# A second, turned copy of w_out for the product with the experts' gate

## The chip, the core and the metric

The kernel runs on one core of a Trainium2 chip. That core has a matrix engine (TensorE: PE for its matmuls, PEld for its weight loads), a vector engine (DVE), a scalar engine (ACT), a general engine (POOL) and a queue engine that issues DMAs (SP). The metric is the device time of one execution in microseconds.

## The reference

Three stages run one after the other. Random-feature attention gives `x`; a gated feed-forward block turns `x` into `h @ w_out`; a router then gives each of 2304 tokens to one of 8 experts, in order of the logits, and each expert has two more matrices.

```
q_p, k_p = phi(q * s), phi(k * s)               # exp of projections, 128 features
num = q_p @ (k_p^T v);  x = num / (q_p . sum k_p)
xn  = x / rms(x) * rms_g
h   = silu(xn @ w_gate) * (xn @ w_val)          # 2304 x 1536
y   = h @ w_out                                 # w_out: 1536 x 512, float64
logits = y @ moe2_w_gate                        # 512 x 8
# tokens to experts by descending logit, at most 288 per expert
out[mask_e] = relu(y[mask_e] @ w1[e]) @ w2[e]
```

`w_out` and the two gate matrices come as float64. The kernel reads their 64-bit words and makes float32 values on the chip.

## The kernel before

**Logits ahead of y.** The router needs the logits exactly and early, and `y` only later. So the kernel computes `wog = w_out @ moe2_w_gate` (1536 x 8) once, and gets the logits as `h @ wog` straight from `h`, as soon as a chunk of `h` is there (`ffn_lg`, L652, L653). `y` itself (L900) is computed afterwards, under the routing.

**Ticks.** `run_tick` (L758) writes one tick of work for each of 88 items: four batches of attention, each 12 items for keys (`KItem`) and 10 for queries (`QItem`). An item is spread over lags 0 to 5 of later ticks. Its TensorE work is projections (L367 to L369; without the split in batch 0, L372), transposes of the features (L454), products with values or keys (L413, L458) and a transpose of the normalised rows (L463). 576 queries make four tiles of 128 rows and one of 64, so in each batch there are two query items (the two halves of the heads) with 64 rows instead of 128; below they are called **half tiles**, and their L454, L458 and L463 read `64*128` or `128*64` in the profile. To each tick belongs one step of the feed-forward (`ffn_step_pe`, 24 matmuls of 256 columns, L596 to L598, called **FFN matmuls** below; 108 such steps in all).

**Conversion.** `useq` (L703) is the list of conversions: 24 `WgvUnit` and then 12 `WoUnit`, one for each chunk of 128 rows of `w_out`. `conv_pe` and `conv_el` move units through lags 0 to 3, one lag per tick; while they convert w_out they start one unit every second tick. All units do `load` (L519, 512 KB into one of three `ws` buffers), at lag 0 `magnitude` (L523, ACT) and at lag 1 `word` (L527, L528, L529, DVE) into one of three `dw` buffers. A `WoUnit` then

- at lag 1 writes the chunk to `wo_dr` in DRAM (L579), from which the product for `y` takes it later (`wo_split`, L816);
- at lag 2 transposes the chunk in four pieces on TensorE (L567) into a PSUM buffer `gv`, from which ACT copies it back over the chunk (L581);
- at lag 3 multiplies the turned chunk with the gate (L571, four matmuls of 8 columns) and puts the two halves of the result into `wog` (L583, L584). `ffn_step_pe` does not go on to a logit product before its chunk is in `wogs`.

The buffers `dw` are shared with `late_load` (L626), which brings the `h` of the first two blocks back for their logits, and the two `gv` buffers with the feed-forward steps.

**Order.** TensorE's order is as written for the first 27 ticks. After that a scheduler in the framework orders all engines' instructions, by priorities (attention ahead of the rest) and by when it expects buffers and operands; each engine then runs its own list strictly in that order.

Of the kernel before, what the change touches and what calls it, by code (L numbers as in the profile page):

```python
# [9 lines left out]
F32 = mybir.dt.float32  # L10
# [10 lines left out]
NT, DM, FF, E, FE = B * S, 512, 1536, 8, 1024  # L21
# [7 lines left out]
KD = DM // 128  # L29
KF = FF // 128  # L30
# [9 lines left out]
DW = 3  # L40
# [14 lines left out]
def const_f32():  # L55
    c = np.zeros((128, C_N), np.float32)
    i = np.arange(128)
    c[:, C_ID:C_SL] = np.eye(128)
    c[:, C_SL:C_SA] = np.arange(SL)
    c[:, C_SA:C_C] = np.arange(NSL)  # L60
    c[:, C_C:C_P] = np.arange(NC)
    c[:, C_P] = i
    c[:, C_E:C_T] = np.arange(E)
    e = np.arange(E)
    c[:, C_T:C_N] = (e[None, :] < e[:, None]).reshape(-1)
    return c


def triangles():
    i = np.arange(128)  # L70
    j = np.tile(np.arange(CAP), (128, 1))
    return np.concatenate([i[:, None] < i[None, :], i[:, None] >= i[None, :], j], 1).astype(np.float32)


def const_i32():
    rows = []
    for n, (d, s) in enumerate(zip(DIGITS, SHIFTS)):
        j = np.arange(1 if n else 2, 1 << d, dtype=np.uint32) << np.uint32(s)
        if n == 0:
            j = np.where(j >= 0x80000000, j ^ np.uint32(0x80000000), ~j)  # L80
        rows.append(j.astype(np.uint32))
    return np.tile(np.concatenate(rows).view(np.int32), (128, 1))
# [195 lines left out]


@with_exitstack  # L280
def kernel(ctx, tc, qT, kT, v1, om, wgv, rms, wo, wg2, w1, w2, cfd, trd, cid, out, dbg=None):
    nc = tc.nc
    dbg = dbg or {}
    keep = ctx.enter_context(tc.tile_pool(name="keep", bufs=1))
# [6 lines left out]
    wo_dr = dram.tile([KF, 128, DM], F32, name="wo_dr")  # L291

    cf = keep.tile([128, C_N], F32, name="cf")
    ident = cf[:, C_ID:C_SL]
# [14 lines left out]
    psG = ctx.enter_context(tc.tile_pool(name="psG", bufs=2, space=PSUM))  # L309
    mid = ExitStack()  # L310
    fp = mid.enter_context(tc.tile_pool(name="fp", bufs=2))
# [54 lines left out]
    def proj(pp, xh, xl):  # L366
        nc.tensor.matmul(pp, xh, omh, start=True, stop=False)  # L367
        nc.tensor.matmul(pp, xh, oml, start=False, stop=False)
        nc.tensor.matmul(pp, xl, omh, start=False, stop=True)  # L369

    def proj_whole(pp, x):
        nc.tensor.matmul(pp, x, oms, start=True, stop=True)  # L372
# [9 lines left out]
    class KItem:  # L382
        def __init__(self, b, p, g):
            self.b, self.p, self.g = b, p, g
            self.ts = [t for t in (2 * g, 2 * g + 1) if t < 5]
# [9 lines left out]
        def pe(self, lag):  # L395
            b, p, g = self.b, self.p, self.g
            if lag == 0:
                self.pp = psA.tile([128, 4, M], F32, name="pp", bufs=2)
                if b == 0:
                    for i, t in enumerate(self.ts):  # L400
                        proj_whole(self.pp[:, 2 * i:2 * i + 2, :], kts[b, p][:, t * 128:t * 128 + 128])
                    return
                kh, kl = khs.pop((b, p, g))
                for i, t in enumerate(self.ts):
                    proj(self.pp[:, 2 * i:2 * i + 2, :], kh[:, i * 128:i * 128 + 128], kl[:, i * 128:i * 128 + 128])
            elif lag == 1:
                if g == 0:
                    st["pk", b, p] = psA.tile([128, 512], F32, name="pm", bufs=3)
                pk = st["pk", b, p]
                vt = vts[b, p]  # L410
                for i, t in enumerate(self.ts):
                    for h in range(2):
                        nc.tensor.matmul(pk[:, h * (D + 1):(h + 1) * (D + 1)], self.ft[:, 2 * i + h, :], vt[:, t, h, :],  # L413
                                         start=(t == 0 and h == 0), stop=(t == 4), skip_group_check=True)

        def el(self, lag):
            b, p, g = self.b, self.p, self.g
            if lag == 0:
                self.ft = feat(self.pp, 128, 2 * len(self.ts))
            elif lag == 1 and g == 2:  # L420
                if p == 0:
                    kvs[b] = at.tile([128, H, D + 1], F32, name="kvs")
                nc.scalar.copy(kvs[b][:, 2 * p:2 * p + 2, :].rearrange("p h d -> p (h d)"),
                               st.pop(("pk", b, p))[:, :2 * (D + 1)])
# [129 lines left out]
                    gvs.add(f)  # L554

    class WoUnit(Unit):
        def __init__(self, f):
            self.f = f

# [1 line left out]
            return wo[self.f]  # L561

        def pe(self, lag):
            if lag == 2:
                self.pt = psG.tile([128, KD, 128], F32, name="gv")
                for k in range(KD):
                    nc.tensor.transpose(self.pt[:, k, :], self.t[:, k * 128:(k + 1) * 128], ident)  # L567
            elif lag == 3:
                self.pw = self.pt[:, 0, :E]
                for k in range(KD):  # L570
                    nc.tensor.matmul(self.pw, self.t[:, k * 128:(k + 1) * 128], wg2s[:, k, :], start=(k == 0), stop=(k == KD - 1))  # L571

        def el(self, lag):
            f = self.f
            if lag == 0:
                self.magnitude(fp.tile([128, DM], F32, name="dw", bufs=DW))
            elif lag == 1:
                self.word()
                nc.sync.dma_start(wo_dr[f], self.t)  # L579
            elif lag == 2:  # L580
                nc.scalar.copy(self.t, self.pt.rearrange("p k m -> p (k m)"))  # L581
            elif lag == 3:
                nc.vector.tensor_copy(wog[:, f, 0, :], self.pw)  # L583
                nc.vector.tensor_sub(wog[:, f, 1, :], self.pw, wog[:, f, 0, :])  # L584
                wogs.add(f)
# [104 lines left out]
    def ffn_step_el():  # L690
        if "el" in fst:
            j, f, pg = fst.pop("el")
            ffn_el(j, f, pg)
            ffn_rank_el()
            return j, f
        return None
# [3 lines left out]
    for b in range(B):  # L700
        items += [KItem(b, p, g) for p in range(4) for g in range(3)]
        items += [QItem(b, t, hf) for t in range(5) for hf in range(2)]
    useq = [WgvUnit(f, g) for f in range(KF) for g in range(2)] + [WoUnit(f) for f in range(KF)]  # L703
    AHEAD = 3


# [126 lines left out]
    while True:  # L833
        if not ffn_step_pe():
            break
        j, f = ffn_step_el()
# [223 lines left out]
def layouts(q, k, v, omega, moe_w_gate, moe_w_val, moe_w_out, moe_rms_g, moe2_w_gate, moe2_w1, moe2_w2):  # L1060
    a = np.asarray
    hp = H // 2

    def bits(x):
        return np.ascontiguousarray(x).view(np.int64)

    qT = a(q).reshape(B, hp, 2, S, D).transpose(0, 2, 4, 1, 3).reshape(B, 128, hp, S)
    kT = np.zeros((B, hp, 128, 640), np.float32)
    kT[..., :S] = a(k).reshape(B, hp, 2, S, D).transpose(0, 1, 2, 4, 3).reshape(B, hp, 128, S)
    v1 = np.zeros((B, hp, 2, 640, D + 1), np.float32)  # L1070
    v1[:, :, :, :S, :D] = a(v).reshape(B, hp, 2, S, D)
    v1[:, :, :, :S, D] = 1.0
    v1 = v1.reshape(B, hp, 2, 5, 128, D + 1).transpose(0, 1, 4, 3, 2, 5)
    om = np.zeros((128, 2 * M), np.float32)
    om[:D, :M] = a(omega).T
    om[D:, M:] = a(omega).T
    wgv = np.stack([bits(moe_w_gate), bits(moe_w_val)], 0).reshape(2, KD, 128, KF, 128).transpose(3, 2, 1, 0, 4)
    wgv = wgv.reshape(KF, 128, 1024)
    rms = np.tile(a(moe_rms_g)[None], (128, 1))
    wo = bits(moe_w_out).reshape(KF, 128, DM)  # L1080
    wg2 = a(moe2_w_gate).reshape(KD, 128, E).transpose(1, 0, 2)
    w1 = a(moe2_w1).reshape(E, KD, 128, 4, 256).transpose(0, 3, 2, 1, 4).reshape(E, 4, 128, 1024)
    w2 = a(moe2_w2).reshape(E, KE, 128, KD, 128).transpose(0, 3, 2, 1, 4).reshape(E, 4, 128, 1024)
    d = dict(qT=qT, kT=kT, v1=v1, om=om, wgv=wgv, rms=rms, wo=wo, wg2=wg2, w1=w1, w2=w2,
             cf=const_f32(), tri=triangles(), ci=const_i32())
    return {n: np.ascontiguousarray(x) for n, x in d.items()}

# [16 lines left out]
```

## Time and profile before

| | |
|---|---|
| median of 3 runs | 1002.11 us (1001.75 to 1002.58) |
| the profiled execution | 998.29 us, of which the span in the profile is 996.5 us |
| PE, PEld busy | 969.5 us (97%), 884.8 us (89%) |
| DVE, ACT, POOL busy | 535.7 us (54%), 399.3 us (40%), 243.7 us (24%) |
| DMA moved | 153.32 MB, mean 154 GB/s |

The span holds three parts: attention with the feed-forward up to about 545 us, routing with the product for `y` under it up to about 750 us, and the experts to the end. A PE row's "busy" is modelled and overlaps with its neighbours, so what a matmul costs is read from one start to the next. PE's idle time is shown by the profile only where a row carries `[idle <-releaser]`.

### The profile page before, as it was taken

What the parts mean: (1) busy time and instruction counts of PE and PEld (TensorE: products, weight loads), DVE (VectorE), ACT (ScalarE), POOL (GpSimd) and SP (SyncE); (2) the same over time, 40 slices, a digit from 0 to 9 for tenths busy, and PEclk for the clock granted to TensorE, in tenths of its full rate; (3) what the DMA queues carried; (4) which work ended last, traced back from release to release, by engine and by line L of the source; (5) the groups of instructions that cost most, each with busy time, mean ns of one, the idle gap of its engine ahead of it and who ended that gap; (6) DMA issues with size and microseconds to landing.
All of it is one profiled execution on the core that took longest, in us unless ns stands there. A gap on an engine that the chain in (4) does not pass through costs nothing.

```text
span 996.5 us, 19333 instructions
## 1 busy us (share of the span) xinstructions
PE 969.5 (97%) x7667; PEld 884.8 (89%) x7667; DVE 535.7 (54%) x1239; ACT 399.3 (40%) x999; POOL 243.7 (24%) x326
## 2 busy tenths in 40 slices
PE   9989999999999999999999999999997999999996
PEld 7788899999999989999999777777776999999996
DVE  4889956454553344432243555655565655555531
ACT  6976545555645545332243011010004544444420
POOL 2456412243444322322232000000005112122111
PEclk9999999999999999999999999999999999999999
DMA  8547744375344111712132666655527855555400
GB/s 299 159 141 234 226 132 125 111 257 199 131 141 155 67 54 51 223 80 86 79 145 107 190 184 178 189 173 166 163 72 239 251 187 183 186 196 198 149 24 24
DMA packets 112074, 153.32 MB, mean 154 GB/s; under 512 B 8560, under 2 KB 78832, under 8 KB 111984
## 3 DMA queue, kind: packets, MB, share of 16 engines
q1 hardware_dynamic: 108768, 142.52, 44.3%
q0 software_dynamic: 3072, 9.44, 2.9%
q8 instruction: 60, 0.98, 0.4%
q14 instruction: 30, 0.25, 0.1%
q10 hardware_dynamic: 144, 0.13, 0.0%
HBM read 108.03 MB, written 44.04 MB: 153 GB/s over the span
## 4 chain that ended last, share of the span: by engine, by line
PE 79%; issue 9%; DVE 6%; DMA 2%; POOL 2%; ACT 2%; POOLq 0%; DVEq 0%; ACTq 0%
PE py L900 16%; PE gv L596 10%; PE gv L597 10%; PE gv L598 9%; PE pm L458 3%; PE cnt L164 2%; PE pm L413 2%; PE py L998 2%; PE py L999 2%; PE ph L988 2%; PE py L1000 2%; PE ph L990 2%; PE ph L989 2%; DVE dw L528 2%; PE pm L454 2%
## 5 line engine op out<-in xcount | busy, mean ns | idle before, releaser
L596 PE MATMUL gv<-xh,wc 128*128 128x256 f32 x864 | 253.3, 293 | 3.1 <-DVE hp L611 2.3
L597 PE MATMUL gv<-xl,wc 128*128 128x256 f32 x864 | 250.4, 290 | 0.1
L598 PE MATMUL gv<-xh,wc 128*128 128x256 f32 x864 | 249.8, 289 | 0.0
L900 PE MATMUL py<-wc,ht 128*128 128x512 f32 x648 | 175.9, 409 | 0.0
L596 PEld LDWEIGHTS gv<-xh,wc 128*128 128x128 f32 x864 | 165.4, 191 | 6.8 <-DVE hp L611 3.3
L597 PEld LDWEIGHTS gv<-xl,wc 128*128 128x128 f32 x864 | 165.5, 192 | 1.3 <-DVE xl L500 0.4
L598 PEld LDWEIGHTS gv<-xh,wc 128*128 128x128 f32 x864 | 165.5, 192 | 0.6
L900 PEld LDWEIGHTS py<-wc,ht 128*128 128x128 f32 x648 | 114.4, 188 | 21.9
L621 POOL TENSOR_TENSOR hp<-h,hp 128x256 fp32r<-128x256 f32 x84 | 65.3, 777 | 164.3 <-ACT hp L620 164.2
L608 DVE SCALAR_TENSOR_TENSOR th<-th,gv 128x256 f32<-128x256 f32 x108 | 45.0, 416 | 112.3 <-ACT th L607 112.1
L379 ACT ACTIVATE ft<-pp,mx 128x128 f32<-128x128 f32 (+1 forms) x320 | 93.5, 372 | 25.5 <-DVE mx L376 23.5
L882 DVE TENSOR_TENSOR wc<-ws,wc 128x1024 fp32r<-128x1024 f32 x58 | 70.9, 1223 | 32.3 <-ACT wc L881 32.3
L607 ACT ACTIVATE th<-gv 128x256 f32<-128x256 f32 x108 | 41.6, 385 | 107.7 <-PE gv L598 107.4
L988 PE MATMUL ph<-exh,wc 128*128 128x288 f32 x256 | 78.3, 307 | 0.0
L998 PE MATMUL py<-ehh,wc 128*128 128x288 f32 x256 | 77.8, 304 | 0.0
L376 DVE TENSOR_REDUCE mx<-pp 128x4 f32<-128x512 f32 (+2 forms) x88 | 55.9, 636 | 37.9 <-PE pp L369 30.7
L999 PE MATMUL py<-ehl,wc 128*128 128x288 f32 x256 | 75.9, 297 | 0.0
L1000 PE MATMUL py<-ehh,wc 128*128 128x288 f32 x256 | 75.8, 296 | 0.0
L990 PE MATMUL ph<-exh,wc 128*128 128x288 f32 x256 | 75.8, 297 | 0.0
L989 PE MATMUL ph<-exl,wc 128*128 128x288 f32 x256 | 75.5, 296 | 0.0
L909 ACT COPY ws<-py 128x512 f32<-128x512 f32 x18 | 10.6, 586 | 145.7 <-PE py L900 131.1
L881 ACT CAST wc<-ws 128x1024 fp32r<-128x1024 f32 x58 | 61.0, 1051 | 3.0 <-DMA ws<-in_w_dram 2.9
(200 smaller groups left out, 1839.0 us busy)
## 6 DMA issues: line engine op xcount, KB each, us to landing
ws<-in_w_dram SPq DMA_DIRECT2D x64, 512.0 KB, 3.6
ht<-h_dr SPq DMA_DIRECT2D x54, 512.0 KB, 4.2
h_dr<-hp SPq DMA_DIRECT2D x42, 512.0 KB, 2.6
ws<-in_wgv_dram SPq DMA_DIRECT2D x24, 512.0 KB, 4.0
ws<-in_wo_dram SPq DMA_DIRECT2D x12, 512.0 KB, 3.8
h_dr<-dw SPq DMA_DIRECT2D x24, 256.0 KB, 2.2
y_dr<-ws SPq DMA_DIRECT2D x18, 256.0 KB, 4.3
vt<-in_v_dram SPq DMA_DIRECT2D x12, 325.0 KB, 4.3
```

The costliest lines, as they stand in the source:

```text
L379: nc.scalar.activation(ft[:n, g], pp[:n, g], AF.Exp, bias=mx[:n, g:g + 1])
L596: nc.tensor.matmul(pg[:, v], w[:, 0, k, v], xh[:, k], start=(k == 0), stop=False)
L597: nc.tensor.matmul(pg[:, v], w[:, 0, k, v], xl[:, k], start=False, stop=False)
L598: nc.tensor.matmul(pg[:, v], w[:, 1, k, v], xh[:, k], start=False, stop=(k == KD - 1))
L882: lo.tensor_sub(w[:, 1], sv, w[:, 0])
L900: nc.tensor.matmul(py, ht[:, i4, a], w[:, l, f % 2], start=(f == 0 and n == 0), stop=(f == KF - 1 and n == 2))
L988: nc.tensor.matmul(ph, w[:, 0, k, m], xh[:, k], start=(k == 0), stop=False)
L989: nc.tensor.matmul(ph, w[:, 0, k, m], xl[:, k], start=False, stop=False)
L990: nc.tensor.matmul(ph, w[:, 1, k, m], xh[:, k], start=False, stop=(k == KD - 1))
L998: nc.tensor.matmul(py, w[:, 0, k], hh[:, k], start=(k == 0), stop=False)
L999: nc.tensor.matmul(py, w[:, 0, k], hl[:, k], start=False, stop=False)
L1000: nc.tensor.matmul(py, w[:, 1, k], hh[:, k], start=False, stop=(k == KE - 1))
```

## The change

The layout on the host now also gives `woT`: each 128 x 512 chunk of `w_out` with its four 128 x 128 pieces turned. A new `WogUnit` loads a chunk of `woT`, converts it with the same `magnitude` and `word`, and at lag 2 multiplies it with the gate. `WoUnit` keeps the load, the conversion and the write to `wo_dr`, and has no TensorE work. The 12 `WogUnit` stand where the `WoUnit` stood in the list, and the 12 `WoUnit` follow them, so the list has 48 units instead of 36, and the pace per tick is the same. The change shifts later line numbers: the FFN matmuls L596 to L598 are L610 to L612 in the new file, and L571 is L588.

```diff
 class WoUnit(Unit):
     def pe(self, lag):
+        pass
+    def el(self, lag):
+        if lag == 0:
+            self.magnitude(fp.tile([128, DM], F32, name="dw", bufs=DW))
+        elif lag == 1:
+            self.word()
+            nc.sync.dma_start(wo_dr[self.f], self.t)
+
+class WogUnit(Unit):
+    def src(self):
+        return woT[self.f]
+    def pe(self, lag):
         if lag == 2:
-            self.pt = psG.tile([128, KD, 128], F32, name="gv")
-            for k in range(KD):
-                nc.tensor.transpose(self.pt[:, k, :], self.t[:, k * 128:(k + 1) * 128], ident)
-        elif lag == 3:
-            self.pw = self.pt[:, 0, :E]
+            self.pw = psG.tile([128, KD, 128], F32, name="gv")[:, 0, :E]
             for k in range(KD):
                 nc.tensor.matmul(self.pw, self.t[:, k * 128:(k + 1) * 128], wg2s[:, k, :], ...)
     def el(self, lag):
...
         elif lag == 1:
             self.word()
-            nc.sync.dma_start(wo_dr[f], self.t)
         elif lag == 2:
-            nc.scalar.copy(self.t, self.pt.rearrange("p k m -> p (k m)"))
-        elif lag == 3:
             nc.vector.tensor_copy(wog[:, f, 0, :], self.pw)
             nc.vector.tensor_sub(wog[:, f, 1, :], self.pw, wog[:, f, 0, :])
             wogs.add(f)
...
-useq = [WgvUnit(f, g) ...] + [WoUnit(f) for f in range(KF)]
+useq = [WgvUnit(f, g) ...]
+useq += [WogUnit(f) for f in range(KF)] + [WoUnit(f) for f in range(KF)]
...
+woT = wo.reshape(KF, 128, KD, 128).transpose(0, 3, 2, 1).reshape(KF, 128, DM)
```

The scheduler also orders the work around it differently. On PE, at the 13th feed-forward step, where the half tile of batch 1 has its feature transposes (L454, out 128x64) and its products with the keys (L458, out 64x65), the program before has them in two blocks:

```order
L598 MATMUL gv<-xh,wc 128x256
L368 MATMUL pp<-oml,qh 128x256
L369 MATMUL pp<-omh,ql 128x256
L454 MATMUL pm<-cf,ft 128x64 x4
L458 MATMUL pm<-kvs,qp 64x65 x4
L596 MATMUL gv<-xh,wc 128x256
```

At the same place the new program has one FFN matmul behind each of them (from the third transpose on):

```order
L454 MATMUL pm<-cf,ft 128x64
L610 MATMUL gv<-xh,wc 128x256
L454 MATMUL pm<-cf,ft 128x64
L611 MATMUL gv<-xl,wc 128x256
L458 MATMUL pm<-kvs,qp 64x65
L612 MATMUL gv<-xh,wc 128x256
L458 MATMUL pm<-kvs,qp 64x65
```

The half tiles thus went from two blocks of four to eight single instructions. Behind batch 0 there are 24 such L454, 24 L458 and 12 L463. Counted over the whole of the two orders, those that stood in blocks before and stand singly now are, by feed-forward step: at 13 four L454 and four L458; at 14 four L458; at 17 four L463; at 41 and at 54 three L454 of four; at 42 four L454 (and the L458 behind them); at 55 two L454. The others stood singly before too, and no such piece went from single to a block.

On PE at the first chunk of w_out, the program before has the transposes of the chunk behind the same batch's products, one feed-forward step later:

```order
L454 MATMUL pm<-cf,ft 128x128 x4
L458 MATMUL pm<-kvs,qp 64x65 x4
L567 MATMUL gv<-cf,dw 128x128 x4
L367 MATMUL pp<-omh,qh 128x256
L368 MATMUL pp<-oml,qh 128x256
```

and the new one has only the product with the gate, ahead of the projections of a query item:

```order
L612 MATMUL gv<-xh,wc 128x256
L588 MATMUL gv<-wg2s,dw 128x8 x4
L367 MATMUL pp<-omh,qh 128x256
L368 MATMUL pp<-oml,qh 128x256
```

The four transposes are gone, and the products stand where a transpose could have stood; full tiles' L454, L458 and L413 stand singly between FFN matmuls more often too. From the 60th feed-forward step on PE's order is the same as before, to the end.

## Rows read from the trace of the kernel before

**Rows 1.** Busy time by stretch: from where PE's order first differs (99.9 us) to the last idle time at the start of the conversion of w_out, the rest of that conversion, the time in which the second half of the list would stand, and the rest up to the last FFN matmul. Columns: stretch, its length, then busy us and instructions of PE, PEld, DVE, ACT, POOL; the granted TensorE clock, DMA share, GB/s.

```profile
99.90:113.90 14.00, 11.89 (x96) 11.23 (x94) 13.83 (x21) 8.88 (x24) 7.80 (x7) 1.00 0.69 216
113.90:246.00 132.10, 131.70 (x1118) 128.44 (x1119) 76.97 (x179) 71.21 (x204) 38.05 (x50) 1.00 0.52 168
246.00:385.00 139.00, 139.00 (x1120) 130.37 (x1120) 58.81 (x156) 69.25 (x216) 51.22 (x77) 1.00 0.32 109
385.00:544.50 159.50, 159.50 (x1338) 156.85 (x1337) 61.94 (x145) 54.50 (x136) 46.08 (x70) 1.00 0.34 117
```

**Rows 2.** PE in order of time, where PE's order first differs, the two longest of PE's waits behind that, and the last FFN matmul. Columns: start us, duration us, engine, line, operation, out<-in, tile, form, count, and idle time before it with its releaser.

```profile
99.90 0.28 PE L597 MATMUL gv<-xl,wc 128*128 128x256 f32 x1
...
106.85 0.44 PE L413 MATMUL pm<-vt,ft 128*128 128x65 f32 x2 [1.40 <-ACT ft L379]
...
113.92 0.39 PE L596 MATMUL gv<-xh,wc 128*128 128x256 f32 x1 [0.72 <-DVE hp L611]
...
544.42 0.28 PE L598 MATMUL gv<-xh,wc 128*128 128x256 f32 x1
```

**Rows 3.** The instructions of the conversion (those that touch a tile `dw`). Columns: line, engine, operation, out<-in, count, then duration in ns (least, median, most), first and last start in us, form.

```profile
L567 PE MATMUL gv<-cf,dw x48: 270/273/327, 128.8 to 245.7; 128*128 128x128 f32 x48
L523 ACT ACTIVATE dw<-ws x36: 658/678/771, 10.1 to 241.2; 128x512 f32<-128x512 f32 x36
L527 DVE TENSOR_SCALAR dw<-dw x36: 387/417/1446, 11.1 to 242.0; 128x512 int32<-128x512 int32 x36
L528 DVE SCALAR_TENSOR_TENSOR dw<-ws,dw x36: 672/693/1714, 11.5 to 242.5; 128x512 int32<-128x512 int32 x36
L529 DVE SCALAR_TENSOR_TENSOR dw<-ws,dw x36: 651/691/1792, 13.0 to 243.2; 128x512 int32<-128x512 int32 x36
L581 ACT COPY dw<-gv x12: 586/589/621, 129.7 to 247.2; 128x512 f32<-128x512 f32 x12
```

**Rows 4.** PE in order of time around the first four transposes of w_out (L567), with a block of half-tile products (L458, two passes each, so x8) ahead of them. Columns as in Rows 2.

```profile
127.50 0.29 PE L369 MATMUL pp<-omh,ql 128*128 128x256 f32 x1
127.62 0.60 PE L454 MATMUL pm<-cf,ft 128*128 128x128 f32 x4
128.15 0.68 PE L458 MATMUL pm<-kvs,qp 128*64 128x65 f32 x8
128.76 0.66 PE L567 MATMUL gv<-cf,dw 128*128 128x128 f32 x4
129.17 0.36 PE L367 MATMUL pp<-omh,qh 128*128 128x256 f32 x1
```

**Rows 5.** PE in order of time at the half tile of batch 1, in two blocks. Columns as in Rows 2.

```profile
122.72 0.28 PE L369 MATMUL pp<-omh,ql 128*128 128x256 f32 x1
122.93 0.46 PE L454 MATMUL pm<-cf,ft 64*128 64x64 f32 x4
123.33 0.68 PE L458 MATMUL pm<-kvs,qp 128*64 128x65 f32 x8
123.94 0.38 PE L596 MATMUL gv<-xh,wc 128*128 128x256 f32 x1
124.16 0.28 PE L597 MATMUL gv<-xl,wc 128*128 128x256 f32 x1
```

**Rows 6.** PE in order of time at a half tile of batch 2: a block of transposes, then products that stand singly between FFN matmuls, and behind them transposes of a full tile that stand singly (L463 `128*128`). Columns as in Rows 2.

```profile
287.21 0.28 PE L369 MATMUL pp<-omh,kl 128*128 128x256 f32 x1
287.42 0.46 PE L454 MATMUL pm<-cf,ft 64*128 64x64 f32 x4
287.81 0.33 PE L458 MATMUL pm<-kvs,qp 128*64 128x65 f32 x2
...
288.38 0.33 PE L458 MATMUL pm<-kvs,qp 128*64 128x65 f32 x2
...
288.95 0.33 PE L458 MATMUL pm<-kvs,qp 128*64 128x65 f32 x2
...
289.79 0.39 PE L596 MATMUL gv<-xh,wc 128*128 128x256 f32 x1
290.01 0.27 PE L463 MATMUL pm<-cf,xn 128*128 128x128 f32 x1
...
290.24 0.27 PE L463 MATMUL pm<-cf,xn 128*128 128x128 f32 x1
```

**Rows 7.** PE in order of time where four transposes of a half tile (L463 `64*128`) stand singly between FFN matmuls. Columns as in Rows 2.

```profile
311.41 0.36 PE L597 MATMUL gv<-xl,wc 128*128 128x256 f32 x1
311.70 0.27 PE L463 MATMUL pm<-cf,xn 64*128 64x64 f32 x1
311.90 0.38 PE L598 MATMUL gv<-xh,wc 128*128 128x256 f32 x1
312.22 0.27 PE L463 MATMUL pm<-cf,xn 64*128 64x64 f32 x1
...
313.46 0.38 PE L598 MATMUL gv<-xh,wc 128*128 128x256 f32 x1
313.68 0.28 PE L596 MATMUL gv<-xh,wc 128*128 128x256 f32 x1
```

**Rows 8.** Waits of the DMA queue (from 165 to 250 us) and of ACT (from 250 to 325 us) for the `dw` buffers and what is loaded into them. Columns: who waited for whom, us in total, times, longest us.

```profile
SPq L628 <- PE gv L571: 15.2, 6, 6.1
ACT dw L636 <- DMA dw<-h_dr: 11.3, 8, 3.6
```

More of the change, by code (lines that the diff above doesn't have):

```diff
@@ L280, with kernel @@
 @with_exitstack
-def kernel(ctx, tc, qT, kT, v1, om, wgv, rms, wo, wg2, w1, w2, cfd, trd, cid, out, dbg=None):
+def kernel(ctx, tc, qT, kT, v1, om, wgv, rms, wo, woT, wg2, w1, w2, cfd, trd, cid, out, dbg=None):
     nc = tc.nc
@@ L563, in pe, with __init__ @@
         def pe(self, lag):
-            if lag == 2:
-                self.pt = psG.tile([128, KD, 128], F32, name="gv")
-                for k in range(KD):
-                    nc.tensor.transpose(self.pt[:, k, :], self.t[:, k * 128:(k + 1) * 128], ident)
-            elif lag == 3:
-                self.pw = self.pt[:, 0, :E]
+            pass
[6 more added lines that the diff above has]
+    class WogUnit(Unit):
+        def __init__(self, f):
+            self.f = f
+        def src(self):
+            return woT[self.f]
+        def pe(self, lag):
+            if lag == 2:
+                self.pw = psG.tile([128, KD, 128], F32, name="gv")[:, 0, :E]
                 for k in range(KD):
@@ L702 @@
         items += [QItem(b, t, hf) for t in range(5) for hf in range(2)]
-    useq = [WgvUnit(f, g) for f in range(KF) for g in range(2)] + [WoUnit(f) for f in range(KF)]
+    useq = [WgvUnit(f, g) for f in range(KF) for g in range(2)]
+    useq += [WogUnit(f) for f in range(KF)] + [WoUnit(f) for f in range(KF)]
     AHEAD = 3
@@ L1083, in layouts @@
     w2 = a(moe2_w2).reshape(E, KE, 128, KD, 128).transpose(0, 3, 2, 1, 4).reshape(E, 4, 128, 1024)
-    d = dict(qT=qT, kT=kT, v1=v1, om=om, wgv=wgv, rms=rms, wo=wo, wg2=wg2, w1=w1, w2=w2,
+    d = dict(qT=qT, kT=kT, v1=v1, om=om, wgv=wgv, rms=rms, wo=wo, woT=woT, wg2=wg2, w1=w1, w2=w2,
              cf=const_f32(), tri=triangles(), ci=const_i32())
```

## The prediction

> **What bounds the kernel now.** I read the busy time by stretch first [rows 1]. From 113.9 us to the last FFN matmul at 544.4 us [rows 2] PE is busy for all but 0.4 us of 430.6 us, and its clock column reads 1.00. DVE has 77.0 of 132.1 us while w_out is converted, 58.8 of 139.0 us behind that. So in this part nothing but PE's own list sets the pace: whatever leaves the list, or makes two neighbours in it dearer, moves everything behind it. Between 99.9 and 113.9 us it is the other way round: DVE is busy 13.83 of 14.00 us and PE waits, 1.40 us for the features and 0.72 us for a block of `h` [rows 2]. What stands on PE there matters less. Behind 544 us the order of PE is the same in both programs, so a shift at 544 us should reach the end as it is.
>
> Busy time does not tell a matmul's price, because the rows overlap: a transpose lasts 273 ns in its row [rows 3], yet four of them take from 128.76 to 129.17 us [rows 4]. I price by starts.
>
> **What is removed.** The 48 transposes: twelve groups of four, 0.41 us from the first one's start to the start of what follows [rows 4], so 12 x 0.41 = **4.9 us** off PE. All of them lie from 128.8 to 245.7 us [rows 3], where PE has no idle time, so all of it is on the path. ACT loses 12 copies of 0.589 us, 7.1 us. The products with the gate (L571) are the same 48 instructions as before, at the same price.
>
> **What is added beside PE.** Twelve more conversions: on ACT 12 x 0.678 = 8.1 us, on DVE 12 x (0.417 + 0.693 + 0.691) = 21.6 us [rows 3], on SP 12 more loads of 512 KB. The pace of one unit in two ticks is kept, so the second twelve stand where the list of before has none, from about 246 to 385 us (24 ticks, about 140 us). DVE has 58.8 us of 139.0 there and goes to about 80, or 58%; ACT goes from 69.3 to 77. What hides them is PE's own work, and the cover has been tried in the same trace: from 113.9 to 246 us DVE is busy 77.0 of 132.1 us, 58% too, with the same conversions in it, and PE is busy 131.70 of 132.10 us [rows 1]. I cost these at nothing. If the cover failed as it does from 99.9 to 113.9 us (DVE at 99%, PE losing 2.1 of 14 us), a stretch of 14 us would cost 2 us. A gain there is excluded, since PE loses nothing in that stretch now.
>
> The chunk of w_out for `y` comes to DRAM later, about 385 us instead of 246. It is first read for the product behind 544 us, so 160 us of PE's work lie between. Cost nothing.
>
> On SP the queue gets 12 more loads and the writes of w_out (L579) stand among late work. SP waits up to 6.1 us for a `dw` buffer now [rows 8], because a unit keeps its buffer from lag 0 to the product at lag 3; in the new code it keeps it to lag 2, and in the second twelve until the write has landed. Behind SP's waits stand the loads of queries and the stores of `h`; ACT waits 11.3 us in eight waits for the returned `h` [rows 8], and PE does not feel it (139.00 of 139.00 us). So I take nothing here, and up to 3 us as the upper bound, about the two waits of rows 2 once more.
>
> **What the new order costs.** This is the term that I did not expect from the diff. Half-tile pieces stand singly between FFN matmuls where they stood in blocks. Their price differs:
>
> - Singly, the four transposes run from 311.41 to 313.68 us: 2.27 us with five FFN matmuls of 0.12 us, and 0.08 us that the product ahead makes the first one start late. That is 1.59 us, **0.40 us each**; one to the next is 0.52 us [rows 7], of which 0.12 is the FFN matmul.
> - A full tile's transposes in the same place are 0.23 us from one to the next [rows 6]; in a block four of them take 0.53 us [rows 4], 0.13 each, and with 0.12 for the FFN matmul that makes 0.25. To interleave full tiles costs nothing.
> - Half-tile products singly are 0.57 us apart [rows 6], so **0.45 us each** besides the FFN matmul.
> - In blocks: from 122.72 to 124.16 us stand four transposes and four products, 1.44 us with two matmuls of 0.12 us [rows 5]: 1.20 us for the eight. A block of products alone takes 0.61 us [rows 4], with its entry about 0.70; a block of transposes 0.40 us [rows 5], with entry and exit about 0.58.
>
> By the two orders: step 13, 4 x 0.40 + 4 x 0.45 - 1.20 = 2.2 us. Step 14, 4 x 0.45 - 0.70 = 1.1 us. Step 17, 1.60 - 0.58 = 1.0 us. Step 42: before, 287.21 to 290.01 us less five matmuls is 2.20 us [rows 6], and it becomes 3.4 us, so 1.2 us. Steps 41 and 54, a block of three and a single: about 0.9 before, 1.6 after, 0.7 us each. Step 55, 0.3 us. Together 7.2 us; I take **7.1 us**, which is what I get when every neighbouring pair in both orders is priced by the median start-to-start time that its kind has in the trace. The same sum makes all other changes of neighbours -0.3 us, and for the program before it gives 442.9 us between the first and last of rows 2, where the trace has 444.5: the 1.6 us that lack are in the main the waits shown in rows 2.
>
> Lower bound of this term: 0, if a switch of shape cost nothing. Upper bound: all 60 half-tile pieces charged in full, 36 x 0.40 + 24 x 0.45 = 25 us, but the order shows which are already single, so I stay with 7.1.
>
> The rule that speaks against this term is in the Trainium skill, "TensorE: Matmul & The Clock Gate", Part 3, The mechanism: PE pulls a weight load ahead of matmuls in flight where it targets other rows or the background buffer, so a small piece between two large ones should hide its load. The trace does not agree: with the full tile it is so (0.23 us), with the half tile it is 0.52 us [rows 6, 7]. By the rule the sum would be about -5 us, by the rows +2.
>
> **Sum.** -4.9 + 7.1 - 0.3 = **+1.9 us** up to 544 us, and the same at the end. The profiled execution of 998.29 us becomes 1000.2 us. It lies 3.8 us under the median of the runs shown, so the prediction for the median is 1002.1 + 1.9 = **1004.0 us**. What a measurement of this kernel can tell from no change is about 0.2%, 2.0 us, so this lies just at that edge.
>
> **Rivals.**
>
> 1. *The waits of before go too.* The 1.40 and 0.72 us [rows 2] and some tenths behind them fall away, because the `gv` buffer that a chunk held from lag 2 to lag 3 is free, and ACT's copies are gone. For it: the two waits are for `gv`'s readers and for ACT. Against it: both lie ahead of the first transpose, where DVE is full, and the instructions on DVE are the same there. +1.9 less 1 to 2 us: 1002.1 to 1003, the same.
> 2. *The second conversion is felt.* DVE is given a `word` of 1.8 us just when it should empty a `gv` buffer, or SP holds back a load behind a write of w_out, and PE waits. It decides from the point where DVE is nearly full, as in the first of rows 1; forecast is 58%. Price by that row: 2.1 us of PE for 14 us; two such stretches make +4, so 1008 us. It is slower.
> 3. *The order costs nothing.* Switching shape is hidden in the new order, and the list gets shorter by 4.9 + 0.3 us: 996.9 us, faster. Against it stand rows 6 and 7 in the same kind of place, with no idle time and no releaser in them.
> 4. *The change does nothing on PE's path*, since something else paces the stretch. Rows 1 speak against it: 1002.1 us, and I give it no chance of its own.
>
> **How the numbers follow.** The forecast has 0.62, spread by some 1 us around +1.9, so half of it on either side of 2.0 us: 0.31 the same, 0.31 slower. Rival 1 has 0.14, all the same. Rival 2 has 0.16, all slower. Rival 3 has 0.08, all faster. Faster 0.08, same 0.45, slower 0.47. The range leaves out rival 3 and the upper half of rival 2 and takes in rival 1: 1001.5 to 1007 us. The likeliest case alone is 1003 to 1005 us.
>
> **What would show it.** In the profile after: no transposes of w_out, and PE without idle time from about 114 us to the last FFN matmul, which starts at about 546 us instead of 544.4. Half-tile pieces at the 13th step 0.52 and 0.57 us apart, with no releaser. DVE about 80 us from 246 to 385 us. It would be wrong if those pieces stood 0.23 us apart (rival 3), if rows of PE behind 246 us carried an idle time (rival 2), or if the stretch behind 546 us had another length than before.

## The result, and the profile after

The changed kernel takes 1012.65 us (median of 4 runs, 1011.98 to 1014.68), the kernel before 1001.93 us in the same job: a ratio of 1.0102, interval 1.0086 to 1.0119. It is slower, by 10.7 us instead of the 1.9 us of the prediction, and above the range. The profiled execution took 1012.36 us.

From the page of the changed kernel: the busy time of each engine over the span, and the clock row (tenths of full clock in 40 slices).

```profile
span 1010.6 us, 19298 instructions
...
PE 980.7 (97%) x7619; PEld 890.3 (88%) x7619; DVE 561.0 (56%) x1275; ACT 399.6 (40%) x999; POOL 246.6 (24%) x326
...
PEclk9979999999999999999999999999998999999998
```

PE lost 48 instructions and is busy 11.2 us longer. That is the reading to stop at: PE's list became shorter, yet it takes longer. The clock row, all 9 before, has a 7 and two 8s. They stand at 51 to 76, 758 to 783 and 985 to 1011 us, where PE's order did not change; two short stretches at the lower clock in the changed part, shown below, still read 9 in slices of 25 us.

The windows by stretch of the changed kernel, columns as in [rows 1]:

```profile
99.90:113.90 14.00, 11.00 (x89) 10.40 (x88) 13.86 (x22) 9.15 (x25) 7.55 (x7) 1.00 0.70 219
113.90:246.00 132.10, 130.07 (x1049) 124.22 (x1048) 76.80 (x175) 62.27 (x184) 37.65 (x50) 0.99 0.45 144
246.00:385.00 139.00, 138.15 (x1073) 127.34 (x1071) 81.38 (x186) 74.62 (x224) 53.51 (x75) 0.99 0.52 176
385.00:557.00 172.00, 172.00 (x1436) 168.45 (x1435) 67.34 (x158) 60.21 (x153) 49.64 (x75) 1.00 0.32 112
```

DVE has 81.4 us between 246 and 385 us, as forecast (80). But PE did 1049 and 1073 matmuls where it did 1118 and 1120 in [rows 1]; 48 of these are the transposes. And there is idle time: 132.10 - 130.07 = 2.03 us and 139.00 - 138.15 = 0.85 us, where [rows 1] give 0.40 and 0.

The last two FFN matmuls, on PE in order of time, changed kernel:

```profile
556.72 0.28 PE L611 MATMUL gv<-xl,wc 128*128 128x256 f32 x1
556.84 0.28 PE L612 MATMUL gv<-xh,wc 128*128 128x256 f32 x1
```

The last starts 12.4 us later than in [rows 2]; 546 us was forecast. To say where, I cut the program by the count of FFN matmuls (24 per step) at the starts of steps 10 and 60, counted from 0. The window between them in the kernel before, and then in the changed kernel:

```profile
108.90:384.10 275.20, 274.09 (x2265) 261.98 (x2264) 140.64 (x340) 142.84 (x427) 92.27 (x129) 1.00 0.42 139
```

```profile
112.90:396.50 283.60, 280.72 (x2216) 263.18 (x2215) 164.53 (x375) 143.00 (x426) 94.91 (x129) 0.99 0.47 156
```

So of the 14.1 us between the two profiled spans, 8.4 lie between step 10 and step 60, 4.0 ahead of step 10, none from step 60 to the last FFN matmul (160.3 us in both), and 1.7 behind it. Of the 4.0 us, 3.6 lie where PE's order is the same in both programs: the place where it first differs is reached at 103.5 us, and at 99.9 us before. The profiled execution of before is 3.6 us under its median, and its mean granted clock is 0.994, where nine later runs of that kernel average 0.990; so the pair shows more than the medians do.

Inside these 283.6 us two things can be read that the sum of the prediction did not have. First the waits of PE between the two steps, the changed kernel (what PE waited for, total us, times, longest):

```profile
PE pm L454 <- ACT ft L379: 1.2, 2, 0.6
PE lg L667 <- POOL hp L635: 0.7, 1, 0.7
PE gv L610 <- DVE hp L625: 0.4, 1, 0.4
PE pm L413 <- ACT ft L379: 0.2, 1, 0.2
```

Second the clock. Windows of the changed kernel: ahead of a stretch at the lower clock, in it and behind it, then ahead of a second one and in it (the granted clock is the third number from the end):

```profile
126.80:130.20 3.40, 3.40 (x19) 2.35 (x19) 0.92 (x4) 1.41 (x5) 0.00 (x0) 1.00 0.93 265
130.20:133.60 3.40, 3.40 (x18) 3.40 (x18) 1.60 (x5) 0.38 (x1) 0.00 (x0) 0.50 0.06 22
133.60:137.00 3.40, 3.40 (x23) 2.62 (x23) 1.04 (x4) 1.62 (x5) 1.28 (x1) 1.00 0.08 17
252.90:256.50 3.60, 2.94 (x20) 2.39 (x21) 3.28 (x10) 3.03 (x11) 0.54 (x2) 1.00 0.42 127
256.50:259.90 3.40, 3.40 (x18) 3.40 (x17) 0.00 (x0) 0.24 (x1) 1.87 (x2) 0.50 0.59 188
```

0.50 is the level of 1.2 GHz. PE ahead of the first and at its start, in order of time:

```profile
127.31 0.27 PE L454 MATMUL pm<-cf,ft 64*128 64x64 f32 x1
127.51 0.38 PE L611 MATMUL gv<-xl,wc 128*128 128x256 f32 x1
127.82 0.33 PE L458 MATMUL pm<-kvs,qp 128*64 128x65 f32 x2
128.08 0.38 PE L612 MATMUL gv<-xh,wc 128*128 128x256 f32 x1
128.40 0.33 PE L458 MATMUL pm<-kvs,qp 128*64 128x65 f32 x2
...
130.74 0.41 PE L611 MATMUL gv<-xl,wc 128*128 128x256 f32 x1
130.96 0.41 PE L612 MATMUL gv<-xh,wc 128*128 128x256 f32 x1
```

The half-tile pieces are the single ones of the prediction, and behind them FFN matmuls start 0.22 us apart instead of 0.12 (from 130.74 to 130.96 us here; from 556.72 to 556.84 us in the rows above). Ahead of the second stretch PE had stood idle for 0.62 us.

### The profile page after: what moved, and what is told of

Its sections match the earlier page's. It is cut to its first block, busy times and chain, and to the rows that moved or that the text cites. A ratio compares the mean times of both kernels' runs of the same rounds, so it can differ in the third digit from the quotient of the medians.

```text
span 1010.6 us, 19298 instructions
## 1 busy us (share of the span) xinstructions
PE 980.7 (97%) x7619; PEld 890.3 (88%) x7619; DVE 561.0 (56%) x1275; ACT 399.6 (40%) x999; POOL 246.6 (24%) x326
## 4 chain that ended last, share of the span: by engine, by line
PE 74%; issue 9%; DVE 7%; DMA 4%; POOL 3%; ACT 1%; POOLq 0%; SPq 0%; DVEq 0%; ACTq 0%
PE py L915 16%; PE gv L610 9%; PE gv L611 9%; PE gv L612 9%; PE pm L458 2%; PE cnt L164 2%; PE py L1013 2%; PE py L1014 2%; PE py L1015 2%; PE pm L413 2%; DVE dw L528 2%; PE ph L1003 2%; PE ph L1005 2%; PE ph L1004 2%; PE pm L454 2%
## 5 line engine op out<-in xcount | busy, mean ns | idle before, releaser
L610 PE MATMUL gv<-xh,wc 128*128 128x256 f32 x864 | 256.1, 296 | 2.2 <-DVE hp L625 1.5
L611 PE MATMUL gv<-xl,wc 128*128 128x256 f32 x864 | 254.5, 295 | 0.1
L612 PE MATMUL gv<-xh,wc 128*128 128x256 f32 x864 | 254.0, 294 | 0.0
L610 PEld LDWEIGHTS gv<-xh,wc 128*128 128x128 f32 x864 | 166.8, 193 | 6.0 <-DVE hp L625 2.1
L612 PEld LDWEIGHTS gv<-xh,wc 128*128 128x128 f32 x864 | 167.2, 194 | 1.3
L379 ACT ACTIVATE ft<-pp,mx 128x128 f32<-128x128 f32 (+1 forms) x320 | 93.8, 371 | 37.9 <-DVE mx L376 37.1
L635 POOL TENSOR_TENSOR hp<-h,hp 128x256 fp32r<-128x256 f32 x84 | 67.4, 803 | 162.7 <-ACT hp L634 162.7
L924 ACT COPY ws<-py 128x512 f32<-128x512 f32 x18 | 10.5, 586 | 142.8 <-PE py L915 129.0
```

The source lines that it names most:

```text
L379: nc.scalar.activation(ft[:n, g], pp[:n, g], AF.Exp, bias=mx[:n, g:g + 1])
L610: nc.tensor.matmul(pg[:, v], w[:, 0, k, v], xh[:, k], start=(k == 0), stop=False)
L611: nc.tensor.matmul(pg[:, v], w[:, 0, k, v], xl[:, k], start=False, stop=False)
L612: nc.tensor.matmul(pg[:, v], w[:, 1, k, v], xh[:, k], start=False, stop=(k == KD - 1))
```

## The experiments

All times are medians in us. "10 to 60" is the window between step 10 and step 60 in the profiled execution; "idle" is its length less PE's busy time; "half" is the time in it at a granted clock of 0.50; "rest" is the length less the idle time and half of "half", so about what the order itself costs; "order" is the difference in the sum of pair prices (the prediction's prices, from 99.9 us to the last FFN matmul) against the program before. Pair prices are good to some 2 us: with the neighbours sorted into kinds in other ways, the same trace gives +3 to +5 us for the changed kernel.

| kernel | median (lowest to highest) | before, same job | ratio, interval | 10 to 60 | idle | half | rest | order |
|---|---|---|---|---|---|---|---|---|
| before | | | | 275.2 | 1.1 | 0 | 274.1 | 0 |
| changed | 1012.65 (1011.98 to 1014.68) | 1001.93 | 1.0102, 1.0086 to 1.0119 | 283.6 | 2.9 | 6.8 | 277.3 | +2.0 |
| e1 one copy | 1005.44 (1003.75 to 1007.62) | 1003.00 | 1.0024, 1.0011 to 1.0037 | 276.2 | 2.5 | 0 | 273.7 | -0.8 |
| e2 extra copy | 1006.12 (1004.86 to 1009.26) | 1003.00 | 1.0037, 1.0023 to 1.0051 | 280.1 | 1.5 | 0 | 278.6 | +4.0 |
| e3 written order, before | 1033.30 (1026.03 to 1036.08) | 1003.00 | 1.0312, 1.0280 to 1.0345 | | | | | |
| e4 written order, changed | 1036.44 (1035.72 to 1039.29) | 1003.00 | 1.0344, 1.0322 to 1.0366 | | | | | |
| e5 late copy | 1004.33 (1002.44 to 1006.30) | 1002.89 | 1.0021, 1.0007 to 1.0034 | 275.8 | 2.6 | 0 | 273.2 | -0.9 |
| e6 whole tiles, changed | 996.83 (994.71 to 1001.91) | 1002.89 | 0.9945, 0.9931 to 0.9959 | 268.5 | 4.5 | 3.4 | 262.3 | -14.0 |
| e7 whole tiles, before | 998.45 (993.74 to 1001.82) | 1002.89 | 0.9949, 0.9928 to 0.9969 | 272.2 | 4.2 | 6.8 | 264.6 | -8.8 |
| e8 whole tiles, late copy | 994.63 (991.57 to 996.12) | 1002.89 | 0.9914, 0.9886 to 0.9942 | 265.9 | 4.4 | 0 | 261.5 | -13.9 |
| e9 changed, again | 1011.30 (1009.61 to 1015.83) | 1001.74 | 1.0094, 1.0080 to 1.0108 | 286.9 | 2.7 | 15.2 | 276.7 | +2.0 |
| e10 product later | 1005.88 (1004.81 to 1006.24) | 1001.74 | 1.0039, 1.0026 to 1.0053 | 280.5 | 1.5 | 6.8 | 275.6 | +2.1 |
| e11 whole, late, later | 991.06 (989.83 to 994.01) | 1002.09 | 0.9888, 0.9862 to 0.9915 | 263.3 | 2.9 | 0 | 260.4 | -13.7 |
| e12 late, later | 1001.79 (998.93 to 1003.36) | 1002.09 | 0.9983, 0.9970 to 0.9996 | 276.5 | 1.1 | 6.8 | 272.0 | -0.7 |

**The two halves of the change.** In e1 the changed kernel lacks the second conversion, and the turned chunk is written to `wo_dr` in its place, so `y` is made with turned chunks; only its time counts.

```diff
 class WogUnit(Unit):
...
         elif lag == 1:
             self.word()
+            nc.sync.dma_start(wo_dr[f], self.t)
...
-useq += [WogUnit(f) for f in range(KF)] + [WoUnit(f) for f in range(KF)]
+useq += [WogUnit(f) for f in range(KF)]
```

> Removal alone: the second twelve conversions are left out, and the turned chunk is what goes to DRAM, so y is made with the turned w_out. Theory A (the second copy crowds DVE, ACT and the dw buffers, TensorE waits and its clock halves): the loss goes, 1000 to 1002 us; the order priced by pairs is 0.8 us shorter than before. Theory B (the loss is in the new order of TensorE and the waits it meets from 110 to 135 us, ahead of the second copy): 1004 to 1008 us, with a half-clock stretch near 130 us still there.

In e2 the kernel before keeps its transposes and gets the second conversion.

```diff
-useq = [WgvUnit(f, g) ...] + [WoUnit(f) for f in range(KF)]
+useq = [WgvUnit(f, g) ...] + [WoUnit(f) for f in range(KF)] + [CopyUnit(f) for f in range(KF)]
```

`CopyUnit` converts and writes the chunk as the new `WoUnit` does, and `WoUnit` no longer writes.

> The added conversions alone: the transposes stay as before, and twelve more conversions of w_out follow, which alone write to DRAM. Theory A: 1008 to 1013 us, with idle time of TensorE and half-clock stretches behind 246 us. Theory B: its order by pairs is 4.0 us longer than before, so about 1006 us, without new half-clock stretches.

Neither half alone is the loss: e1 is 2.4 us over before, e2 3.1 us, the whole 10.7. Both times are those of theory B, but its stretch at the lower clock near 130 us did not come in e1. The second conversion alone made PE wait little more (idle 1.5 us, 1.1 before); its cost, 4.9 us between the steps, is nearly all order: by the pair prices +4.0, since half-tile pieces stand singly there too. The removal alone did not gain the 4.9 us that its transposes had cost.

**Is it the planner's order alone?** (The planner is the framework's scheduler.) e3 and e4 keep TensorE's order as written until tick 60 instead of 27, in the kernel before and in the changed one (`FIXED = 60`).

> The kernel before with TensorE's order as written for 60 ticks instead of 27. By pairs 1.7 us shorter than before. Both theories: 1000 to 1002 us if TensorE meets no wait; it is the partner of the next run.

> The changed kernel with TensorE's order as written for 60 ticks instead of 27. By pairs 2.4 us shorter than its partner (the transposes' 5.2 us less half tiles' 2.8 us). Theory A: 5 us or more above its partner, since the second copy is the same. Theory B: 998 to 1000 us, 2 to 3 us below its partner.

Both missed by over 30 us, so they say nothing on the difference. They show a price. The waits of PE in e3, between 112 and 400 us, and then those in e4:

```profile
PE gv L567 <- DVE dw L529: 17.6, 6, 3.3
```

```profile
PE gv L588 <- DVE dw L529: 15.9, 5, 3.2
```

As written, what needs the converted chunk stands on PE one tick behind the conversion's start, and waits for its third DVE instruction. In e4 the clock falls at the end of each of the five waits, for 6.8 us; in e3 it falls at three of the six, for 3.4 us. The window of the first wait of e4 and the one behind it:

```profile
194.00:196.10 2.10, 0.00 (x0) 0.00 (x0) 2.00 (x3) 0.32 (x1) 1.12 (x1) 1.00 0.00 0
196.10:200.00 3.90, 3.88 (x18) 3.88 (x19) 0.76 (x3) 1.03 (x3) 0.73 (x1) 0.51 0.55 168
```

**The place of the second copy.** e5 leaves all in the changed kernel, but the twelve `WoUnit` are written behind attention, one for each feed-forward step.

```diff
-useq += [WogUnit(f) for f in range(KF)] + [WoUnit(f) for f in range(KF)]
+useq += [WogUnit(f) for f in range(KF)]
...
+useq += [WoUnit(f) for f in range(KF)]
...
+    conv_pe(1)
...
+    conv_el()
```

> The changed kernel with the twelve conversions for y moved behind attention, one to each feed-forward step, where TensorE has only FFN matmuls and DVE is 38% busy. By pairs its order is 2.8 us shorter than the changed kernel's (half tiles 22.3 us instead of 25.1). Theory A (the loss comes from the second copy standing among attention: through the order, the waits and the clock): 1002 to 1005 us. Theory B (the loss comes with the removal and its order, ahead of the second copy): 1009 us or more.

8.3 us of the loss went with it, as theory A has it. But the twelve did not run behind attention: the planner moved them forward again. Their first step (L523) from 256 us on, in the changed kernel and then in e5:

```profile
L523 ACT ACTIVATE dw<-ws x12: 648/672/685, 264.6 to 350.6; 128x512 f32<-128x512 f32 x12
```

```profile
L523 ACT ACTIVATE dw<-ws x12: 655/674/716, 325.3 to 377.1; 128x512 f32<-128x512 f32 x12
```

Attention's features (L379) go on to 402 us in e5, so e5 shows what a later and closer place beside attention does ("late" means that below). There PE never waits, with DVE busy 78% of the time:

```profile
325.00:381.00 56.00, 56.00 (x451) 52.62 (x451) 43.80 (x93) 31.75 (x95) 19.25 (x24) 1.00 0.67 213
```

Between the steps there is no stretch at half clock, and the order is cheaper too (-0.9 instead of +2.0). PE's waits stay (2.6 us).

**Half tiles.** e6 and e7 compute the half tiles as whole ones with 64 zero rows, in the changed kernel and in the one before, so no 64-row piece is left.

```diff
+            if n < 128:
+                nc.gpsimd.memset(qt, 0.0)
...
-        n = q_tiles(b)[t][1]
+        n = 128
...
```

> The changed kernel with its half tiles computed as whole ones (64 rows of zeros are added and thrown away), so that no matmul of attention has another shape than its neighbours. If a half tile between FFN matmuls costs 0.40 and 0.45 us, the order is 16 us shorter by pairs: 995 to 999 us. If that price is not on the path, 1010 to 1014 us.

> The same edit in the kernel before. By pairs 8.8 us shorter than before: 992 to 996 us. If the price is not on the path, 1001 to 1004 us.

More columns, and faster: the changed kernel gains 15.8 us, the one before 4.4. With whole tiles the changed kernel is the faster by the medians (996.83 against 998.45), but their runs overlap. e6 lies where it was expected, and e7 missed by some 2 us: it gained half of its 8.8 us of order. In its profile PE waits 3.83 us for features at 303 us, with 6.8 us at half clock. e8 is e6 with the late copy:

> Whole tiles and the late copy together, in the changed kernel: by pairs 15.8 us shorter than the changed kernel. If both causes add up: 987 to 991 us, faster than both kernels. If whole tiles take away what the late copy would, 995 to 999 us.

The time lies between the two expectations, 3.6 us above the one and 0.4 us below the other. The late copy takes 2.2 us off e6, where it took 8.3 us off the changed kernel: with whole tiles most of that gain is not there to be had. PE idles as long as in e6 (4.4 and 4.5 us between the steps).

**Again, and the product one tick later.** e9 is the changed kernel without an edit. e10 moves the product of the turned chunk:

```diff
 class WogUnit(Unit):
...
     def pe(self, lag):
-        if lag == 2:
+        if lag == 3:
...
-        elif lag == 2:
+        elif lag == 3:
             nc.vector.tensor_copy(wog[:, f, 0, :], self.pw)
```

> The changed kernel without any edit, beside the next run on the same chip. Question: are the two stretches at half clock at 130 and 256 us of the changed kernel's profile a property of its order, or of one lucky or unlucky run? Theory A (a property of the order: PE waits at the same places in each run and the clock falls behind them): the median comes out at 1011 to 1014 again, a mean granted clock of 0.982 to 0.986, and the profile has stretches at 0.5 behind the waits at 120 and 254 us again, a step 10 to step 60 time of 283 to 284 us. Theory B (the place where the clock falls varies from run to run): a median of 1005 to 1010, and 279 to 281 us from step 10 to step 60 where no such stretch lies in it.

> The changed kernel with the product of the turned chunk one tick later (lag 3 instead of 2), so that it stands further behind the conversion that it waits for; its PE order has the same sum of pair prices (444.8 us from 99.9 us to the last FFN matmul). Theory A (waits in front of the half-clock stretches are what costs beyond the order): the wait at about 254 us for the converted chunk and the half-clock stretch behind it go, 2 to 4 us less than the changed kernel in the same job: 1008 to 1011. Theory B (the stretches come from elsewhere, the wait of 0.9 us there is no cause): same as the changed kernel to within 1.5 us.

e9 repeats the time as theory A has it (1011.3 us), and not the 283 to 284 us between the steps (286.9). Three of PE's waits are a property of the program. PE's instructions with idle time from 227 to 254 us in e9:

```profile
229.04 0.44 PE L413 MATMUL pm<-vt,ft 128*128 128x65 f32 x2 [0.23 <-ACT ft L379]
...
230.71 0.29 PE L667 MATMUL lg<-hp,wog 128*16 128x256 f32 x1 [0.67 <-POOL hp L635]
...
251.94 1.10 PE L454 MATMUL pm<-cf,ft 128*128 128x128 f32 x4 [0.61 <-ACT ft L379]
```

The changed kernel's profile has the same three, 1.5 us later, of 0.23, 0.67 and 0.62 us. Its other two (0.37 and 0.62 us, at 117 and 120 us) are not in e9, which has two at 328 us (0.69 and 0.22). The places of the half clock differ: behind the wait at 252 us the clock of e9 does not fall, against theory A. Windows of e9, ahead of and in two of its stretches:

```profile
122.50:125.90 3.40, 3.40 (x18) 2.22 (x17) 1.85 (x4) 1.17 (x5) 0.00 (x0) 1.00 0.78 155
125.90:132.70 6.80, 6.80 (x31) 6.12 (x31) 2.71 (x7) 0.79 (x3) 0.81 (x1) 0.50 0.21 77
...
368.30:371.70 3.40, 3.40 (x18) 2.22 (x17) 0.00 (x0) 1.41 (x5) 0.07 (x1) 1.00 0.00 0
371.70:375.10 3.40, 3.40 (x16) 3.26 (x17) 1.44 (x5) 0.38 (x1) 0.00 (x0) 0.50 0.02 5
```

In e10 all three waits are gone, and the time with them: 5.4 us less than e9 on the same chip, more than the 2 to 4 expected, with the same sum of pair prices. The window 225 to 260 us, in the changed kernel and then in e10:

```profile
225.00:260.00 35.00, 33.40 (x263) 31.64 (x262) 17.05 (x38) 16.51 (x48) 13.57 (x16) 0.95 0.53 183
```

```profile
225.00:260.00 35.00, 35.00 (x303) 34.55 (x302) 21.98 (x50) 19.32 (x55) 16.30 (x20) 1.00 0.61 203
```

What changed on ACT can be read in the rows of who waited for the product (engine and line, us, times), in the changed kernel and then in e10:

```profile
  ACT dw L523: 4.9, 5
```

```profile
  ACT dw L523: 1.2, 3
```

L523 is the first step of a conversion, and the features (L379) stand on the same engine. But these five waits do not lead to PE's three: they end at 149, 162, 194, 214 and 235 us, and PE's at 230.5, 232.2 and 253.5 us. Ahead of the first of the three a chain can be read, on ACT and then on PE of the changed kernel:

```profile
229.13 0.68 ACT L523 ACTIVATE dw<-ws 128x512 f32<-128x512 f32 x1 [0.41 <-PE lg L667]
229.82 0.41 ACT L342 CAST kh<-kt 128x256 fp32r<-128x256 f32 x1
230.13 0.36 ACT L379 ACTIVATE ft<-pp,mx 128x128 f32<-128x128 f32 x1
```

```profile
230.54 0.44 PE L413 MATMUL pm<-vt,ft 128*128 128x65 f32 x2 [0.23 <-ACT ft L379]
```

A conversion, which had itself waited for a `dw` buffer, stands ahead of the features that PE waits for. At 253.5 us no conversion stands just ahead of the features on ACT. The runs show that the lag is the cause, not each link.

**Both cures.** e11 is e8 with the product at lag 3, e12 is e5 with it.

> The changed kernel with whole tiles and the late second copy as before, and with the product of the turned chunk one tick later as well (lag 3). The sum of pair prices is 429.1 us, against 429.0 with the product at lag 2. Theory A (the product at lag 2 makes PE wait for the converted chunk, and the waits between 200 and 240 us, 1.7 us in the run with lag 2, go with it): 992 to 994 us, with no idle time of PE between 180 and 250 us. Theory B (those waits are for the logits' own reads and not for the product): 994 to 996.5 us, the waits at their places.

> The changed kernel (half tiles as they are) with the late second copy and the product one tick later. Theory A: the waits at 208 and 241 us of the run with the late copy alone (1.5 us) go, 1002 to 1003.5 us. Theory B: 1004 to 1006 us. If the sum by order, waits and half clock holds, the time from step 10 to step 60 is that of the program before, 275.2 us, within 1 us, with no stretch at half clock in it.

Both came out as theory A has it or slightly better: e11 is 3.6 us faster than e8 (in another job, against nearly the same time of before), and it beats the kernel before by 11 us. e12 has the time of the kernel before to 0.3 us. The waits at 208 and 241 us are gone. Its sum missed: 276.5 us between the steps instead of 275.2 within 1 us, with 6.8 us at half clock where none was expected, 3.4 us behind half-tile pieces at 151.5 us and as much at 359.7 us.

## Why the prediction was wrong

**The step that failed: PE's list was priced as if it ran at full clock, and without waits.** The prediction read "its clock column reads 1.00" and "PE is busy for all but 0.4 us" from the kernel before, took both over to the new order, and had no term for either. Two things came on top of the order's price.

*The clock.* The mean granted clock is known of each run, not only of the profiled ones. An estimate of the time lost to the lower clock is the span times what that mean lacks to 1, averaged over the runs: 15.4 us for the changed kernel (e9, five runs) and 10.0 us for the kernel before in the same job (nine runs). So about 5.4 of the 9.6 us lie there, with some 1.5 us of uncertainty. In the two profiles the part between the steps is 3.4 and 7.6 us (half of "half"). e10 loses 13.7 us in that way, so 1.7 of the 5.4 us that it gains on e9 are clock. With the second copy late nearly nothing of the difference is left: e5 loses 11.6 us against 10.9 in its job, e12 11.9 against 11.2. Neither half of the change shows it alone: e1 loses 12.1 and e2 10.5 us, against 11.6.

*The waits.* PE idles 2.9 and 2.7 us between the steps instead of 1.1. In the kernels with half tiles the waits go with the tick of the product, and not with the second copy: at lag 2 there are 2.5 to 2.9 us of idle time, with the second copy early (the changed kernel, e9), late (e5) or left out (e1); at lag 3 there are 1.1 to 1.5 us (before, e2, e10, e12). With whole tiles e8 and e11 differ in the same way (4.4 and 2.9 us), but e7, at lag 3, has 4.2 us. So **"The products with the gate are the same 48 instructions as before, at the same price"** held for PE's list and not for its waits: e10 shows that having them one tick earlier costs 5.4 us, e5 against e12, from two jobs, some 2 us with the late copy.

**"I cost these at nothing", of the conversions beside PE,** held for PE's waits and not for the time. DVE's share came out as forecast, 81.4 of 139 us, DVE is nowhere full, and while the second twelve run PE is busy 90.85 of 91.00 us in the changed kernel:

```profile
264.00:355.00 91.00, 90.85 (x725) 84.43 (x723) 61.34 (x136) 52.62 (x157) 38.34 (x55) 1.00 0.59 199
```

Besides their part in the clock, what they cost is PE's order: "rest" is 3.5 to 4.5 us longer with them early than with them late or without them (the changed kernel and e9 against e5, e10 against e12, e2 against before), and with whole tiles 0.8 us (e6 against e8). With them early the half tiles of batches 2 and 3 stand singly: the first run of L454 and L458 in batch 2 takes 3.9 us from first to last in the changed kernel, e2, e9 and e10, and 2.2 us in before, e1, e5 and e12. The prediction had 2.9 us of this in its sum, at steps 41 to 55, as the new order's price and not as theirs.

Rival 2 got 0.16 and the price of 1008 us. Its condition, "from the point where DVE is nearly full", is wrong: DVE at 78% costs PE no wait in e5. Its sign came, idle time of PE behind 246 us (0.62 us), but the waits are 1.6 to 1.8 of the 10.7 us. Its price was 4.6 us low, and had nothing for the clock. Rival 1's waits did not go: the 1.40 us for the features became 1.86 us, the 0.72 us for `h` became 0.37 us.

**"What the new order costs"** held. The pieces stand 0.52 and 0.57 us apart with no releaser (127.31, 127.82, 128.40 us), as forecast. So the rule of the Trainium skill that the prediction weighed ("TensorE: Matmul & The Clock Gate", Part 3, The mechanism), from which it took that a small piece hides its load, does not agree with this trace either. Without idle time and half clock, "rest" is 3.2 and 2.6 us over before in the two profiles of the changed kernel, where the prices give 2.0; in the nine other kernels of the table that have both, "rest" and "order" agree within 2.2 us, where "order" goes from -14.0 to +4.0. What no price held: the clock also fell with no idle time. Of the nine such stretches that begin between step 10 and step 60 in the profiles of the changed kernel, e9, e10 and e12, eight (all but 256.5 us) begin inside a run of half-tile pieces or within 2.5 us behind its end, and none lies in the whole-tile kernels except within 2 us of an idle time of PE. But e5 has such a run of pieces at the same step, and before at 355 us, and both kept the clock; and the number of stretches differs between two runs of one program.

**"12 x 0.41 = 4.9 us off PE"** is half shown. e6 against e7 has the removal with no half tiles in the way, and by the prices -5.2 us; the window is 3.7 us shorter, "rest" 2.3 us, the median 1.6 us. With the copy late as well (e8 against e7) "rest" is 3.1 us shorter, and with half tiles (e12 against before) 2.1 us. (The stretch where PE "has no idle time" had 0.40 us of it [rows 1].) e1 gained nothing: its order is 0.8 us cheaper instead of 5.2, because the order around it moved.

**Account for the median's 10.7 us.** From the table: order +2.6 to +3.2 (by "rest"; the sum had +1.9), idle +1.6 to +1.8, half clock +3.4 to +7.6 in the two profiles, together 8.4 and 11.7 us between the steps. The clocks of all runs give the same picture: 9.6 us less 5.4 us leaves 4.2 us for order and waits. The 2x2 of cures, from three jobs in which before took 1001.7 to 1002.9 us: 1011.3 (e9), 1005.9 with the product later, 1004.3 with the late copy, 1001.8 with both. So the two edits together take the loss away, and their gains do not add: 5.4 and 7.0 us singly, 9.5 together. Why they overlap is not shown.

**What stays open.** Why the clock falls at a run of half-tile pieces in one execution and not in the next: the places and the price are read, the cause is not, and about half of the loss hangs on it. The late start of step 10 (112.9, 110.7 us in the two profiles, 108.9 before): the stretch at half clock at 65 us is 10.2 us long in one, 3.4 in the other and in before, and 6.8 in the eleven other kernels' profiles, so it comes and goes with the run. The part behind the last FFN matmul is 452.1 us in before and 452.6 to 456.1 in the kernels with "10 to 60" above; no experiment touched it. It too may be the clock: the stretches at half clock from 750 to 800 us are 3.4 us in before (452.1 us), 6.8 in the changed kernel (453.7) and 13.6 in e9 (456.1). And of the links between lag 2 and PE's waits, one is read and the others are not.

**"A shift at 544 us should reach the end as it is"** held within 1.7 us in the first profile and 4.0 us in e9. The late write of `wo_dr` and the added loads on SP cost nothing that shows: in e5 they come still later, and the time is less.

## What to carry to other kernels

When work is put beside an engine that is the bound, the helper's busy share does not say whether it is hidden: look at what it does to the bound engine's list and to its waits. Here PE never waited beside DVE at 78%, and lost time at 58%, where the planner had set half tiles singly. Do not take the clock of the old order over to a new one: compare the mean granted clock of several runs, since one profile can show a lucky run. Check in the trace where a planner put the work that an edit moved. A step made shorter by one tick can take away the slack that a planner's order needed (5.4 us here).

Price neighbours by their starts: here odd-shaped pieces cost more as singles than the columns that they save. Padding them to whole tiles (with the second copy later and its product one tick later) made a kernel with the change 1.1% faster than before (whole tiles alone 0.5%) instead of 1.0% slower.

## What was not expected of the hardware

The clock fell to 1.2 GHz where the profile shows PE busy without a gap: 126.8 to 130.2 us has PE busy 3.40 of 3.40 us, and PEld 2.35. Those two numbers do not foretell it: e5 and then the kernel before, at a like run of half-tile pieces, read the same, and both have a granted clock of 1.00 from there to step 60.

```profile
124.80:128.20 3.40, 3.40 (x18) 2.22 (x17) 1.16 (x3) 1.41 (x5) 0.00 (x0) 1.00 0.85 219
```

```profile
354.90:358.30 3.40, 3.40 (x18) 2.20 (x17) 1.16 (x3) 1.72 (x6) 0.70 (x1) 1.00 0.37 144
```

Whole tiles with 64 useless rows are faster than half tiles: 998.45 against 1002.89 us in the kernel before, with eight query items of 64 rows made 128.
